# Eight experts as one straight program at fixed sizes, with one weight ring and transposed outputs

## The chip, the cores and the metric

The kernel runs on one core of one Trainium2 chip. The core has a matrix engine (TensorE, PE in the rows, with its weight loads as PEld), a vector engine (VectorE, DVE), a scalar engine (ScalarE, ACT), GpSimd (POOL) and SyncE (SP), which here only issues DMAs. The metric is the device time of one execution in microseconds. The kernel before took 626.72 us (median of three runs: 617.67, 628.06, 626.72).

## The reference, cut to what matters

Three layers follow one another on 1152 tokens of 512 features (2 batches of 576, 8 heads of 64):

```
attn = g * (phi(q) M_prev / phi(q) z_prev) + (1 - g) * causal_softmax(q k^T / 8) v

logits = x @ w_gate;  expert = argmax(logits);  gate = max of softmax(logits)
a token is kept if it is among the first 288 of its expert; else its output row is 0
out[i] = gate[i] * relu(x[i] @ w1[e]) @ w2[e]          # 8 experts, 512 -> 1024 -> 512

xn = x / sqrt(mean(x^2) + 1e-6) * rms_g
y  = (silu(xn @ w_gate2) * (xn @ w_val)) @ w_out        # 512 -> 1536 -> 512
```

All is float32. With the reference's default draw the experts have 14, 151, 0, 60, 1, 556, 8 and 362 tokens, so after the limit of 288 the sorted counts are 288, 288, 151, 60, 14, 8, 1, 0, together 810 rows. The rows of the third layer are these 810; the other tokens' output is 0.

## The kernel before, in words

**Precision.** Large products are made of three matmuls on a split into a high part (rounded to the matrix engine's fast float format, fp32r) and a low part (the rest): hi*hi, hi*lo, lo*hi (TERMS). For expert weights the split is a cast and a subtraction (`split`, L853 and L854). The weights of the third layer are read as 32-bit words in pairs (their high and low words) and put together by bit operations before the same split (`conv_steps`, L767 to L785): of one 1 MB matrix four pieces, each with three ACT, four DVE and one POOL instruction. Small products are plain float32 matmuls from the raw weights.

**Attention** (L188 to L712) is straight code with a written order; its end routes the tokens: each block's rows are scattered with a gate factor and a token number behind the 512 features into `disp`, a DRAM table with 288 rows for each expert. `rank` orders the experts by their counts on the DVE; the loads of expert weights take their addresses from registers on SP. Some weights are loaded (seven buffers of 1 MB, `wraw`) and two are split already here.

**Experts** (L1126 to L1317). There are eight positions in order of work: largest, smallest, second smallest, second largest, third smallest, third largest, and so on. For each position every engine reads a class number (the count rounded up to 0, 32, 64, 128, 160, 256 or 288 rows, and whether the next one is tiny) and jumps with `tc.Switch` (L1201) into the arm written for that class. An arm above 64 rows (`up_big`, L987; `down`, L1014) multiplies with split weights; the hidden layer comes out with its 1024 features on the partitions, the output with tokens on the partitions, by 128 rows and a tail of 32 (`down_tail`, `gather`). An arm of 32 or 64 rows (`tiny`, L941) uses float32 matmuls. What finishes an expert (`finish_y`, L1053: sum of squares, root, scaling, and a DMA to `comp`, the compact table of rows) is for most positions in a second switch after the arm (`finish_later`, L1067). Weights come through the seven buffers in an order of their own for each position (`uses`, `seq`, `ring`); three matrices of the third layer are loaded and converted inside expert arms (`extra`). The work of PE, DVE, ACT and POOL inside an arm is in written order.

**Third layer** (L1318 to L1487). It is one more switch, with an arm for each number of 64-row half blocks. 832 rows are in three chunks of 256, 256 and 320 columns. For each of six groups of 256 hidden features and each chunk, `gv` makes gate and value (48 matmuls a chunk and group), then `outp` multiplies into the output rows. Rows are read from `comp` (`x_in`), normalised, turned on PE (`x_turn`) and split. All engines but PE and SP are ordered here by a scheduler. Finished rows are scattered into the output by token number.

Of the kernel before, what the change touches and what calls it, by code (L numbers as in the profile page):

```python
# [22 lines left out]
def attn_moe_kernel(ctx, tc, q, k, v, M_prev, z_prev, beta, w_gate, w1, w2, cap, g_gate, g_val, g_out, rms_g, out):  # L23
# [21 lines left out]
    nc.gpsimd.memset(zrow[:, DM:DM + 1], 1.0)  # L45
# [11 lines left out]
    CW = DM + 2  # L57
    EB = 5
# [3 lines left out]
    comp = dram.tile([N + P * max(NBK, 2), CW], F32, name="comp")  # L62
# [33 lines left out]
    def rank(pk, erow):  # L96
# [5 lines left out]
        nc.vector.tensor_scalar(out=up, in0=ra, scalar1=-2.0, scalar2=float(2 * E - 1), op0=ALU.mult, op1=ALU.add)  # L102
        nc.vector.scalar_tensor_tensor(out=ra, in0=ra, scalar=2.0, in1=up, op0=ALU.mult, op1=ALU.min)
        nc.vector.tensor_scalar(out=up, in0=ra, scalar1=-2.0, scalar2=1.0, op0=ALU.mult, op1=ALU.add)
        nc.vector.scalar_tensor_tensor(out=up, in0=ra, scalar=2.0, in1=up, op0=ALU.is_lt, op1=ALU.mult)
        nc.vector.tensor_tensor(out=ra, in0=ra, in1=up, op=ALU.add)
# [11 lines left out]
    extra = {0: [0], 3: [1], 5: [2]}  # L118
    succ = lambda e: 2 if e == 0 else e + 1
    uses = [[] if e == 1 else [4 * e + 2, 4 * e + 3] + [4 * E + u for u in extra.get(e, [])] + ([4 * succ(e), 4 * succ(e) + 1] if e + 1 < E else []) for e in range(E)]  # L120
    seq = [0, 1] + [u for e in range(E) for u in uses[e]]
    early = seq[:NRAW]
    pos = {u: i for i, u in enumerate(seq)}
    SK = 4 * E + sum(len(z) for z in extra.values()) - len(seq)

    X2 = pos[4 * (E - 2) + 3]
    ring = [(X2 + j) % NRAW for j in (1, 2, 3, 4, 5, 0, -1)]

    def raw_tile(u):
        i = pos.setdefault(u, u - SK)  # L130
        if i < NRAW and i not in rawt:
            rawt[i] = wraw.tile([P, HALF], F32, tag="wr", name="wr")
        return rawt[i % NRAW if i < X2 + NRAW else ring[(i - X2 - NRAW) % NRAW]]

# [27 lines left out]
    wctx = ExitStack()  # L162
# [28 lines left out]
    ctx.enter_context(tc.manual_schedule(engines={mybir.EngineType.PE, mybir.EngineType.SP}))  # L191
    with ExitStack() as actx:
# [288 lines left out]
        def route(b, i, x):  # L481
# [39 lines left out]
            nc.vector.reciprocal(out=x[:n, DM:DM + 1], in_=r4[:n, 3:4])  # L521
# [89 lines left out]
        def act(z):  # L611
# [93 lines left out]
        for u in early[NRAW - 2:]:  # L705
            wl[u] = w_load(u // 4, u % 4) if u < 4 * E else m2_load(u - 4 * E)
# [7 lines left out]
    m2w = ctx.enter_context(tc.tile_pool(name="m2w", bufs=3, reuse_waits="tile"))  # L714
# [6 lines left out]
    sizes = sorted({min(s, cap) for s in [0, 32, 64, P] + [j * P + r for j in range(1, NBK) for r in (32, P)]})  # L721
    NS = len(sizes) - 1
    SM = 32
    NT = sum(s <= 2 * SM for s in sizes) - 1
    LO0 = sum(s < min(cap, -(-N // E)) for s in sizes)
    HI1 = sum(s < min(cap, N // E) for s in sizes)
    assert LO0 > NT
    arms = [[(c, t) for t in (False, True) for c in range(NS + 1)]] * E
    never = lambda e, c, t: e == 0 and c < LO0 or e == 1 and c > (NT if t else HI1)
    sthr = mc.tile([P, E, NS], F32, name="sthr")  # L730
    for j, s in enumerate(sizes[:-1]):
        nc.gpsimd.tensor_scalar(out=sthr[:, :, j], in0=ebase, scalar1=float(s), scalar2=None, op0=ALU.add)
    ccmp = pcmp.rearrange("p a b -> p (a b)")[:, :E * NS].rearrange("p (e s) -> p e s", e=E)

    rg_sb = mc.tile([P, DM], F32, name="rg_sb")
    nc.sync.dma_start(rg_sb, rms_g[None, :].to_broadcast([P, DM]))
    cnt = mc.tile([P, E], F32, name="cnt")
    off = mc.tile([P, E], F32, name="off")
    tmp = mc.tile([P, E], F32, name="tmp")
    tot = mc.tile([P, 1], F32, name="tot")  # L740
    ctl = mc.tile([P, 2, E], I32, name="ctl")
    ctt = mc.tile([P, 4], I32, name="ctt")
    nc.gpsimd.memset(eps, 1e-6)
    flg = mc.tile([P, E], F32, name="flg")
# [83 lines left out]
    with ExitStack() as mctx:  # L828
# [685 lines left out]
```

## Time and profile before

| what | value |
|---|---|
| median of the three runs | 626.72 us |
| lowest, highest run | 617.67, 628.06 us |
| profiled execution, first to last instruction | 621.6 us |
| PE, DVE, ACT, POOL busy | 77%, 55%, 44%, 28% of the span |

The profiled execution is one more run of its own; for it the span is the time that is listed, and it lies inside the range of the three runs. The rows below give times in us from the span's start. Attention ends near 199 us, the first matmul of the third layer starts at 420 us.

### The profile page before, as it was taken

Reading aid. Unit: us, or ns where it says so; the run is one execution under the profiler, and the core shown is the slowest. Engines: PE = TensorE matmul, PEld = TensorE weight load, DVE = VectorE, ACT = ScalarE, POOL = GpSimd, SP = SyncE. Lnnn points to the kernel's source line nnn. Section 1 sums busy time; section 2 is a strip of 40 time slices with the busy share of each in tenths; the row PEclk is TensorE's granted clock in tenths of the full one; section 3 lists DMA queues with packets and bytes.
Section 4 is the critical chain, followed back from the end, with each engine's and each line's share of the span. In section 5 each row is a group of like instructions: output and inputs, shape, how many; then the busy total and the mean of one; then the engine's idle time right before and its main releaser. Section 6 shows DMA issues by size and latency. Waiting matters only on the chain.

```text
span 621.6 us, 11099 instructions
## 1 busy us (share of the span) xinstructions
PE 478.9 (77%) x3753; PEld 399.2 (64%) x3754; DVE 342.5 (55%) x943; ACT 274.9 (44%) x704; POOL 173.0 (28%) x275
## 2 busy tenths in 40 slices
PE   7679999798984882455845683375998899999995
PEld 4568878687864751255534551234897788898993
DVE  6736754667575820217322460022799898989432
ACT  5736655465562620315322430123677565655210
POOL 3122321424162410224223420000146152434113
PEclk9879997898896996677975787668899999999998
DMA  9899695704964473463667443422965540000002
GB/s 170 159 289 235 148 223 117 155 2 112 322 220 128 137 251 73 158 196 135 210 180 224 147 144 95 116 65 64 388 213 172 198 152 37 1 2 1 1 35 76
DMA packets 76152, 89.33 MB, mean 144 GB/s; under 512 B 39862, under 2 KB 49078, under 8 KB 75873
## 3 DMA queue, kind: packets, MB, share of 16 engines
q1 hardware_dynamic: 73792, 81.25, 44.8%
q0 software_dynamic: 1936, 5.32, 2.5%
q14 instruction: 223, 1.82, 1.2%
q8 instruction: 57, 0.93, 0.8%
q10 hardware_dynamic: 144, 0.00, 0.0%
HBM read 61.90 MB, written 14.41 MB: 123 GB/s over the span
## 4 chain that ended last, share of the span: by engine, by line
issue 22%; DVE 16%; PE 9%; DMA 4%; ACT 4%; POOL 3%; SPq 1%; another core or an unknown queue 0%; ACTq 0%; DVEq 0%; POOLq 0%
DVE wr L774 3%; DVE t L769 3%; DMA wr<-in_moe_w 2%; POOL mlo L785 2%; PE gv L825 2%; DVE t L776 2%; DVE t L778 1%; DVE acc L1419 1%; DVE gh L1399 1%; DMA wr<-in_moe_w_gate 1%; PE z L1412 1%; PE keep L975 1%; DVE s L1396 1%; ACT t L767 1%; DVE wl L854 1%
## 5 line engine op out<-in xcount | busy, mean ns | idle before, releaser
L785 POOL TENSOR_TENSOR mlo<-t,mhi 128x256 fp32r<-128x256 f32 x72 | 66.2, 944 | 108.4 <-ACT mhi L784 83.3
L825 PE MATMUL gv<-XT,mhi 128*128 128x320 f32 (+1 forms) x384 | 82.2, 298 | 4.2 <-ACT s L1395 3.3
L999 PE MATMUL hpb<-xh,wh 128*128 128x288 f32 (+1 forms) x192 | 49.9, 350 | 36.1 <-issue 18.9
L825 PEld LDWEIGHTS gv<-XT,mhi 128*128 128x128 f32 x384 | 63.3, 189 | 7.4 <-ACT s L1395 5.0
L999 PEld LDWEIGHTS hpb<-xh,wh 128*128 128x128 f32 x192 | 40.1, 244 | 38.5 <-issue 19.6
L1412 PE MATMUL z<-mhi,gh 128*128 128x512 f32 (+1 forms) x168 | 60.5, 407 | 2.8 <-DVE acc L1419 1.3
L410 PE MATMUL s<-k,qT 128*128 128x256 f32 (+2 forms) x256 | 49.3, 318 | 10.5 <-DMA qT<-w 10.5
L443 DVE TENSOR_REDUCE nm<-s 128x1 f32<-128x384 f32 (+4 forms) x60 | 38.9, 648 | 33.2 <-PE s L413 19.5
L825 PE MATMUL gv<-XT,mlo 128*128 128x256 f32 (+1 forms) x192 | 56.7, 295 | 0.0
L479 PE MATMUL o<-rv,pt 128*64 128x65 f32 (+1 forms) x800 | 47.0, 240 | 0.0
L767 ACT ACTIVATE t<-wr 128x256 f32<-128x256 f32 x72 | 29.9, 440 | 38.3 <-DVE wr L774 34.6
L449 ACT ACTIVATE p<-s,nm 128x128 f32<-128x128 f32 (+4 forms) x80 | 42.9, 561 | 6.7 <-PE t L464 3.2
L410 PEld LDWEIGHTS s<-k,qT 128*128 128x128 f32 (+1 forms) x256 | 37.9, 195 | 12.2 <-issue 11.3
L479 PEld LDWEIGHTS o<-rv,pt 128*64 128x64 f32 (+1 forms) x800 | 37.2, 147 | 8.9 <-issue 5.2
L468 ACT COPY pt<-t 128x512 f32<-128x512 f32 (+2 forms) x48 | 23.9, 497 | 36.8 <-PE t L464 36.6
L464 PE MATMUL t<-ident,p 128*128 128x128 f32 (+2 forms) x240 | 37.9, 283 | 2.2 <-DVE phT L341 2.1
L1412 PEld LDWEIGHTS z<-mhi,gh 128*128 128x128 f32 (+1 forms) x168 | 30.9, 184 | 12.1 <-DVE xs L1419 1.9
L825 PE MATMUL gv<-xs,mhi 128*128 128x256 f32 x176 | 34.4, 287 | 4.3 <-DVE XT L1381 4.3
L825 PEld LDWEIGHTS gv<-XT,mlo 128*128 128x128 f32 x192 | 36.2, 189 | 1.0
L951 PE MATMUL hps<-wr,xf 128*32 128x256 f32 (+1 forms) x112 | 15.4, 607 | 26.3 <-issue 25.0
L774 DVE SCALAR_TENSOR_TENSOR wr<-wr,t 128x256 uint32<-128x256 uint32 x72 | 35.6, 526 | 0.1
L769 DVE TENSOR_SCALAR t<-wr 128x256 uint32<-128x256 uint32 x72 | 30.6, 455 | 8.7 <-POOL mlo L785 6.3
(287 smaller groups left out, 1073.8 us busy)
## 6 DMA issues: line engine op xcount, KB each, us to landing
wr<-in_moe_w SPq DMA_DIRECT2D x28, 1024.0 KB, 6.5
wr<-in_moe_w_gate SPq DMA_DIRECT2D x6, 1024.0 KB, 7.1
wr<-in_moe_w_val SPq DMA_DIRECT2D x6, 1024.0 KB, 9.5
wr<-in_moe_w_out SPq DMA_DIRECT2D x6, 1024.0 KB, 10.1
disp<-zrow SPq DMA_DIRECT2D x4, 1040.0 KB, 11.0
k<-w SPq DMA_DIRECT2D x8, 512.0 KB, 7.1
xs<-disp SPq DMA_DIRECT2D x12, 260.0 KB, 4.5
qT<-w SPq DMA_DIRECT2D x12, 256.0 KB, 6.5
```

Of the source, the lines that this page charges most:

```text
L410: nc.tensor.matmul(dst[:n, o0:o0 + c1 - c0], lhsT=st[b, i]["qT"][:, h, st[b, i]["off"]:st[b, i]["off"] + n], rhs=kT[b][half][j][:, h, k0:k ...
L443: nc.vector.tensor_reduce(out=m, in_=s.rearrange("p (g w) -> p g w", g=g)[:n, :, :ext], axis=AX.X, op=ALU.max, negate=True)
L449: nc.scalar.activation(out=p[:n, a * w:a * w + ext], in_=s[:n, a * w:a * w + ext], func=AF.Exp, bias=m[:, a:a + 1], scale=1.0)
L464: nc.tensor.transpose(tv[:kr, a * nk + j, :n], p[:n, a * w + j * P:a * w + j * P + kr], ident[:n, :n])
L479: nc.tensor.matmul(o[c:c + 64, h % 4], lhsT=pt[:kr, a + j, c:c + 64], rhs=vs[b, j][:kr, h], start=(j == 0), stop=(j == i))
L767: nc.scalar.activation(out=t1, in_=H.bitcast(F32), func=AF.Square)
L769: nc.vector.tensor_scalar(out=t2, in0=H, scalar1=0xC0000000, scalar2=None, op0=ALU.bitwise_and)
L774: nc.vector.scalar_tensor_tensor(out=H, in0=H, scalar=3, in1=t1.bitcast(U32), op0=ALU.logical_shift_left, op1=ALU.bitwise_and)
L785: nc.gpsimd.tensor_tensor(out=lo[:, s_], in0=f, in1=hi[:, s_].bitcast(F32), op=ALU.subtract)
L825: nc.tensor.matmul(pss[part], lhsT=W[wi][:, o:o + P], rhs=XT[:, a, k_, c0:c0 + n] if m0 else XT0[a][k_ // 2][:, k_ % 2, :n], start=(k_ == ...
L999: nc.tensor.matmul(ps[:, :un], lhsT=W[k_ // (KD // 2)][w][:, c:c + P], rhs=xh[:, a, k_, :un], start=(k_ == 0 and n_ == 0), stop=(k_ == KD ...
L1412: nc.tensor.matmul(zs[m][:nr], lhsT=h[:, a, r:r + nr], rhs=W[wi][:, fi * DM:(fi + 1) * DM], start=(fi == 0 and n_ == 0), stop=(fi == 1 and ...
```

## The change

The attention part stays, but for two details: the gate factor is multiplied into the row before it is scattered, and `rank` deals the positions anew. Positions are now large, small, large, small, large, small, and then two small ones: 1st, 8th, 2nd, 7th, 3rd, 6th, 4th, 5th in order of count. Each position has a fixed number of rows (`ROWS`), whatever its count. The three large ones and the five small ones are written one after the other without a switch; a small expert's steps are called between the steps of the large one ahead of it (hooks). What does not fit is done by one general arm behind a single flag (`overflow`). All 32 expert matrices and then the third layer's matrices pass through the ring of seven in one order (`pump`, `done`).

Outputs have their features on the partitions: `down` makes 128 features by n tokens, the sum of squares over features is a matmul with ones (`fin_norm`), and `fin_put` writes columns into `compT` and token numbers into `idsD`. The third layer reads its input turned already. Its first three matrices are converted after the last expert, into the buffers of the experts' split weights.

```diff
-    CW = DM + 2
-    EB = 5
+    ROWS = [min(cap, r) for r in (cap, 32, cap, 32, 192, 32, 64, 32)]
+    CPAD = cap + P
...
-            nc.vector.reciprocal(out=x[:n, DM:DM + 1], in_=r4[:n, 3:4])
+            nc.vector.reciprocal(out=r4[:n, 3:4], in_=r4[:n, 3:4])
+            nc.vector.tensor_scalar(out=x[:n, :DM], in0=x[:n, :DM], scalar1=r4[:n, 3:4], scalar2=None, op0=ALU.mult)
...
-    arms = [[(c, t) for t in (False, True) for c in range(NS + 1)]] * E
-    never = lambda e, c, t: e == 0 and c < LO0 or e == 1 and c > (NT if t else HI1)
...
+        def pump():
+            while loaded[0] < min(len(seq), 4 * E + NRAW) and loaded[0] - NRAW in gone:
+                u = seq[loaded[0]]
+                wl[u] = w_load(u // 4, u % 4) if u < 4 * E else m2_load(u - 4 * E)
+                loaded[0] += 1
+
+        def done(*us):
+            gone.update(us)
+            pump()
...
+                nc.scalar.copy(hi[:, s_], t[:, s_])
+                nc.vector.tensor_tensor(out=lo[:, s_], in0=t[:, s_], in1=hi[:, s_].bitcast(F32), op=ALU.subtract)
+                if j:
+                    done(u)
+                yield
...
+            for d in range(KD):
+                ps = ps_h.tile([P, 512], F32, tag="h", name="ypb")
+                for f in range(KF):
+                    c = (f % (KF // 2)) * DM + d * P
+                    for n_, (a, w) in enumerate(TERMS):
+                        nc.tensor.matmul(ps[:, :n], lhsT=W[2 + f // (KF // 2)][w][:, c:c + P], rhs=ht[:, a, f, :n], start=(f == 0 and n_ == 0), stop=(f == KF - 1 and n_ == 2))
+                nc.scalar.activation(out=sq[:, d, :n], in_=ps[:, :n], func=AF.Square)
+                nc.vector.tensor_scalar(out=yg[:, d, :n], in0=ps[:, :n], scalar1=rgT[:, d:d + 1], scalar2=None, op0=ALU.mult)
+                hook(d)
...
+        def fin_norm(e):
+            _, yg, n, pl, s = fin[e]
+            ps = ps_x.tile([P, 512], F32, tag="x", name="ssp")
+            nc.tensor.matmul(ps[:, :n], lhsT=onesf, rhs=s, start=True, stop=True)
+            nc.scalar.activation(out=s, in_=ps[:, :n], func=AF.Sqrt, scale=1.0 / DM, bias=eps)
+            nc.vector.reciprocal(out=s, in_=s)
+            nc.vector.tensor_tensor(out=yg, in0=yg, in1=s.unsqueeze(1).to_broadcast([P, KD, n]), op=ALU.mult)
...
+        def put(off_, row, n, yg):
+            nc.gpsimd.dma_start(compT.rearrange("(k p) n -> p k n", p=P)[:, :, bass.ds(off_, n)], yg)
+            nc.gpsimd.dma_start(idsD[bass.ds(off_, n), :], disp[bass.ds(row, n), DM + 1:DM + 2])
...
-            for a in tc.Switch({g_: cls_v[e] if nxt else end_v for g_ in AE}, len(arms[e])):
-                cls, flag = arms[e][a]
...
+        for e in BIGS:
+            t, nx, pv = e + 1, e + 2 if e + 2 in BIGS else None, e - 1 if e else None
+            bg = Steps(split(u) for u in (4 * e + 2, 4 * e + 3))
+            def up_hook(f):
+                if f == 0 and e:
+                    fin_norm(e - 2)
+                    fin_put(e - 2)
+                    fin_put(e - 1)
+                bg(1)
+                if f == 4:
+                    t_turn(t, xl[t][0], ROWS[t])
+            up(e, up_hook)
+            bg()
+            t_up(t, ROWS[t], raw4(t))
+            done(4 * t, 4 * t + 1)
+            sp = Steps(split(u) for u in (4 * nx, 4 * nx + 1)) if nx else Steps()
+            def down_hook(d):
+                if d == 0:
+                    t_mid(t, ROWS[t])
+                elif d == 1:
+                    t_down(t, ROWS[t], raw4(t))
+                    done(4 * t + 2, 4 * t + 3)
+                elif d == 2:
+                    t_fin(t, ROWS[t])
+                else:
+                    fin_norm(t)
+                if nx and d < len(tks(nx)):
+                    x_turn(nx, d)
+                sp(2 if d == 1 else 1)
+                if d == 3:
+                    fin_sum(e)
+            down(e, down_hook)
+            sp()
...
+        t_turn(6, xl[6][0], ROWS[6])
+        t_up(6, ROWS[6], raw4(6))
+        done(24, 25)
+        fin_norm(4)
+        fin_put(4)
+        w2ctx.close()
+        ovp = pool("ovp", 1)
+        xst = fbp.tile([P, KD, cap], F32, name="sq")[:, :, :2 * P]
+        nc.gpsimd.dma_start(xst, compT.rearrange("(k p) n -> p k n", p=P)[:, :, :2 * P])
+        fin_put(5)
+        t_mid(6, ROWS[6])
+        t_turn(7, xl[7][0], ROWS[7])
+        t_down(6, ROWS[6], raw4(6))
+        done(26, 27)
+        t_up(7, ROWS[7], raw4(7))
+        done(28, 29)
+        t_fin(6, ROWS[6])
+        t_mid(7, ROWS[7])
+        t_down(7, ROWS[7], raw4(7))
+        done(30, 31)
+        fin_norm(6)
+        fin_put(6)
+        t_fin(7, ROWS[7])
+        fin_norm(7)
+        fin_put(7)
...
+        for u in range(2):
+            Ms[u] = m2_conv(wl[4 * E + u], msets[u])
+        g01 = [ps_y[1 - fi].tile([P, 2, 2 * P], F32, tag="y", name="g0") for fi in range(2)]
+        gv_mm((0, (0, 2), 0), 2 * P, Ms, [g01[0][:, part] for part in range(2)], None)
...
+        for a in tc.Switch({g_: flag_v for g_ in AE}, 2, hint="over"):
+            if a:
+                overflow()
+        tc.switch_hint({g_: nb_v for g_ in AE}, 2 * MT - NH0 + 1, "nb")
+        gv_mm((0, (0, 2), 1), 2 * P, Ms, [g01[1][:, part] for part in range(2)], None)
+        Ms[2] = m2_conv(wl[4 * E + 2], msets[2])
...
+            for c in chunks[1:]:
+                c0, n = c[0] * P, ncol(c)
+                nc.sync.dma_start(stage(c), compT.rearrange("(k p) n -> p k n", p=P)[:, :, c0:c0 + n])
...
-        for a in tc.Switch(nb_v, 2 * MT):
+        for a in tc.Switch(nb_v, 2 * MT - NH0 + 1, hint="nb"):
```

The helpers `t_turn`, `t_up`, `t_mid`, `t_down` and `t_fin` are the steps of a small expert (`tiny` before, cut in five), `x_turn` and `up` are `x_turn_in` and `up_big` without their tails. How the change moves instructions, at two places:

The first is PE at the last two small experts (`hps` and `tps` are a small expert's hidden layer and output, `hx`, `xps`, `yx` turned tiles, `ssp` the sum of squares). Before, one of the arms of 32 rows:

```order
L1506 UNCONDITIONAL_BRANCH
L1201 BRANCH_PREFETCH_HINT
L1506 UNCONDITIONAL_BRANCH
L880 MATMUL xps<-ident,ht 128x128 x4
L951 MATMUL hps<-wr,xf 32x256 x16
L964 MATMUL hx<-ident,h 128x128 x2
L975 MATMUL keep<-wr,h 32x128 x32
L887 MATMUL xps<-ident,xs 128x128 x8
```

Now, from the end of the third large expert on:

```order
L931 MATMUL ssp<-ssum,onesf 128x32
L952 MATMUL xps<-ident,xs 128x64 x4
L965 MATMUL tps<-wr,xf 64x512 x8
L931 MATMUL ssp<-ssum,onesf 128x192
L976 MATMUL hx<-ident,h 128x128 x4
L952 MATMUL xps<-ident,xs 128x32 x4
L991 MATMUL tps<-wr,h 64x256 x16
L965 MATMUL tps<-wr,xf 32x256 x16
L1001 MATMUL yx<-ident,ysb 128x128 x2
L976 MATMUL hx<-ident,h 128x128 x2
L991 MATMUL tps<-wr,h 32x128 x32
```

A small expert's matmuls are the same; the branches around them are gone, and the two last small experts run side by side with no large one to fill their gaps.

The second is DVE at the conversion of the third layer's matrices (L769 to L778 before, L761 to L770 now). Before, inside the arm of a large expert, between the hidden layer's low parts (`ht`):

```order
L1010 SCALAR_TENSOR_TENSOR ht<-hpb,ht 128x256
L769 TENSOR_SCALAR t_4548<-wr 128x256
L769 TENSOR_SCALAR t_4553<-wr 128x256
L774 SCALAR_TENSOR_TENSOR wr<-wr,t_4547 128x256
L774 SCALAR_TENSOR_TENSOR wr<-wr,t_4552 128x256
L1010 SCALAR_TENSOR_TENSOR ht<-hpb,ht 128x256
L776 SCALAR_TENSOR_TENSOR t_4548<-wr,t_4548 128x256
L776 SCALAR_TENSOR_TENSOR t_4553<-wr,t_4553 128x256
L778 SCALAR_TENSOR_TENSOR t_4548<-wr,t_4548 128x256
```

Now, behind the last small expert's normalisation:

```order
L933 RECIPROCAL ssum<-ssum 128x32
L934 TENSOR_TENSOR tyg<-tyg,ssum 128x4x32
L1098 TENSOR_LOAD ctl
L1099 TENSOR_LOAD ctl
L1100 SWITCH_STRIDE
L1100 ISA
L1100 BRANCH_PREFETCH_HINT
L1104 TENSOR_TENSOR xh<-sq,xh 128x2x256 x2
L761 TENSOR_SCALAR t_4473<-wr 128x256
L761 TENSOR_SCALAR t_4478<-wr 128x256
L766 SCALAR_TENSOR_TENSOR wr<-wr,t_4472 128x256
```

Three conversions, which lay in the expert stage, now stand behind it.

## Rows read from the trace of the kernel before

**Rows 1.** Busy time by stage: experts, then the third layer in two stretches.

```profile
core 0: us, PE busy (x) PEld busy (x) DVE busy (x) ACT busy (x) POOL busy (x), PEclk, DMA share, GB/s
...
199.00:420.00 221.00, 132.28 (x854) 98.67 (x856) 68.53 (x112) 62.91 (x169) 50.38 (x62) 0.76 0.48 154
420.00:463.00 43.00, 34.47 (x221) 31.22 (x218) 27.68 (x71) 25.08 (x64) 9.88 (x18) 0.92 0.67 239
463.00:581.00 118.00, 112.25 (x716) 100.46 (x715) 107.75 (x269) 72.82 (x195) 47.79 (x49) 1.00 0.22 75
```

**Rows 2.** Waits, 199 to 420 us: engine, line, releaser, us in total, times, longest.

```profile
PEld hps L951 <- issue: 33.8, 22, 12.6
```

**Rows 3.** Chain of waits, 199 to 420 us: shares by line.

```profile
by line: issue 42.5%; DMA wr<-in_moe_w 6.9%; PE keep L975 3.2%; DVE wl L854 2.7%; SPq L868 2.3%; PE yps L975 2.2%; PE hpb L999 1.8%; DMA comp<-xn 1.5%; ACT h L1056 1.4%; PE keep L1023 1.3%; PE yps L1023 1.3%; DVE t L769 1.1%; DVE ht L1010 1
```

**Rows 4.** Timeline, expert stage begins: start, us, instruction, idle before and its releaser.

```profile
192.98 0.95 DVE L890 TENSOR_TENSOR xh<-xps,xh 128x512 fp32r<-128x512 f32 x2 [0.16 <-ACT xh L889]
...
198.98 0.60 PE L999 MATMUL hpb<-xh,wh 128*128 128x288 f32 x1 [5.67 <-issue]
...
202.97 0.38 PE L999 MATMUL hpb<-xh,wl 128*128 128x288 f32 x1
```

**Rows 5.** PE timeline: 18 matmuls of 288 columns, 21 of 192, four transposes.

```profile
213.60 0.43 PE L999 MATMUL hpb<-xh,wh 128*128 128x288 f32 x2
...
216.00 0.43 PE L999 MATMUL hpb<-xh,wh 128*128 128x288 f32 x2
...
216.53 0.60 PE L880 MATMUL xps<-ident,xs 128*128 128x128 f32 x4
...
343.18 0.39 PE L999 MATMUL hpb<-xh,wh 128*128 128x192 f32 x2
...
345.53 0.39 PE L999 MATMUL hpb<-xh,wh 128*128 128x192 f32 x2
```

**Rows 6.** PE timeline: small experts of 32 and 64 rows, third layer's first matmul.

```profile
246.64 3.64 PE L951 MATMUL hps<-wr,xf 128*32 128x256 f32 x32 [12.14 <-issue]
...
261.41 3.48 PE L975 MATMUL keep<-wr,h 128*32 128x128 f32 x64
...
402.72 6.23 PE L951 MATMUL hps<-wr,xf 128*64 128x512 f32 x16 [7.56 <-issue]
...
415.34 5.06 PE L975 MATMUL yps<-wr,h 128*64 128x256 f32 x32
...
420.33 0.39 PE L825 MATMUL g<-xs,mhi 128*128 128x256 f32 x1
```

**Rows 7.** DVE timeline: half of a split with POOL idle.

```profile
258.97 1.22 DVE L854 TENSOR_TENSOR wl<-wr,wh 128x1024 fp32r<-128x1024 f32 x1
```

**Rows 8.** Weight DMAs (count, KB, us to landing), and a stretch full of loads.

```profile
wr<-in_moe_w SPq DMA_DIRECT2D x28, 1024.0 KB, 6.5
...
432.00:448.00 16.00, 14.14 (x84) 12.78 (x84) 10.54 (x28) 9.55 (x26) 2.25 (x6) 0.79 0.98 357
```

**Rows 9.** Stages as in rows 1, only instructions on the raw weights (`wr`).

```profile
420.00:463.00 43.00, 2.07 (x16) 1.44 (x12) 19.48 (x50) 5.38 (x14) 0.43 (x3) 0.92 0.67 239
463.00:581.00 118.00, 0.00 (x0) 0.00 (x0) 76.88 (x197) 19.16 (x47) 0.00 (x0) 1.00 0.22 75
```

**Rows 10.** PE timeline: first matmul of the sixth and last group.

```profile
581.23 0.28 PE L825 MATMUL gv<-xs,mhi 128*128 128x256 f32 x1
```

**Rows 11.** ACT and PE behind the last switch: idle before, and releaser.

```profile
430.44 1.28 ACT L1395 ACT_TABLE_LOAD   x1 [7.99 <-issue]
...
L1378 PEld LDWEIGHTS xgp<-ident,wr 128*128 128x128 f32 x8 | 0.9, 141 | 3.5 <-issue 3.5
```

**Rows 12.** Result rows' DMAs: count, KB, us to landing.

```profile
comp<-xn POOLq DMA_DIRECT2D x6, 64.2 KB, 2.5
```

**Rows 13.** Matmuls by shape, 199 to 445 us: 192 columns, small experts of 32.

```profile
L999 PE MATMUL hpb<-xh,wh 128*128 128x192 f32 x64 | 17.6, 370 | 15.0 <-DVE ht L1010 7.7 <-issue 7.3
...
L951 PE MATMUL hps<-wr,xf 128*32 128x256 f32 x96 | 9.2, 549 | 18.8 <-issue 17.4 <-ACT gi L1058 1.4
```

More of the change, by code (lines that the diff above doesn't have):

```diff
@@ L117, in attn_moe_kernel @@
     rawt = {}
[L118 to L127, printed above, removed]
+    early = list(range(NRAW))
     def raw_tile(u):
[L130 to L133, printed above, removed]
+        if u < NRAW and u not in rawt:
+            rawt[u] = wraw.tile([P, HALF], F32, tag="wr", name="wr")
+        return rawt[u % NRAW]
     def w_load(e, part, t=None):
@@ L806, in m2_conv @@
         return hilo
[L808 removed]
     ps_y = [ctx.enter_context(tc.tile_pool(name=f"ps_y{j}", bufs=1, reuse_waits="tile", space=PSUM)) for j in range(2)]
[L810 to L813 removed]
     TERMS = ((0, 0), (0, 1), (1, 0))
+    xh = xh[0]
+    XT0 = xh[:, :, :, :2 * P]
+    msets = [[W[s][a][:, c * UE:(c + 1) * UE] for a in range(2)] for s in range(2) for c in range(2)]
+    Ms = {}
     def gv_mm(u, n, M, pss, XT):
@@ L841, in attn_moe_kernel @@
+        w2ctx = ExitStack()
+        wsp = w2ctx.enter_context(tc.tile_pool(name="wsp2", bufs=1, reuse_waits="tile"))
         W.extend([wsp.tile([P, HALF], F32R, name=f"w{a}{s}") for a in ("h", "l")] for s in range(2, 4))
         ht = htp.tile([P, 2, KF, cap], F32R, name="ht")
-        SPLIT = (("ap", "vv"), ("ap", "av"))
-        SPLIT0 = (("ap", "ap"), ("ap", "ap"))
         SC = HALF // 2
-        def split(u, plan=None, ahead=True):
+        BIGS = [e for e in range(E) if e % 2 == 0 and e <= 4]
@@ new lines, in attn_moe_kernel, with __init__, __call__ @@
+        ld = nc.values_load_multi_w_load_instructions
+        class Steps:
+            def __init__(self, gens=()):
+                self.g = list(gens)
+            def __call__(self, n=99):
+                while n and self.g:
+                    if next(self.g[0], 0) == 0:
+                        self.g.pop(0)
+                    else:
+                        n -= 1
+        seq = [*range(4 * E), *(4 * E + u for u in range(3 * NG))]
+        gone, loaded = set(), [NRAW]
+        def pump():
[3 more added lines that the diff above has]
+                loaded[0] += 1
@@ L1123, in attn_moe_kernel @@
-        mw = [[m2w.tile([P, UE], F32R, name=n_) for n_ in ("mhi", "mlo")] for _ in range(3)]
-        Ms = dict(enumerate(mw))
-        def background(gens):
-            gens = list(gens)
-            def bg(n):
-                while n and gens:
-                    if next(gens[0], 0) == 0:
-                        gens.pop(0)
-                    else:
-                        n -= 1
-            return bg
-        ld = nc.values_load_multi_w_load_instructions
+                    nc.tensor.matmul(yps[i * nr:(i + 1) * nr, :dw], lhsT=htf[:, hc:hc + nr], rhs=ws[2 + f // (KF // 2)][:, o + i * dw:o + (i + 1) * dw], start=(f == 0), stop=(f == KF - 1))
```

713 lines of the change are left out of this document (215 added, 498 removed).

## The prediction

> **What bounds the kernel now.** I read the stages first, then the waits and the chain of the middle stage, then single timelines. By stage [rows 1], PE is busy 132 of 221 us in the experts at a mean granted clock of 0.76, and 147 of 161 us in the third layer up to its last group, at 0.92 and 1.00. So the loss lies in the experts. There the longest waits name no engine and no transfer: PE's weight load at L951 alone waited 33.8 us for "issue" [rows 2], which is time in which an engine that waits for nothing has no instruction to run, and "issue" is 42.5% of the chain of that stage, about 94 us [rows 3]. The waits stand where an arm begins: 5.67 us before the first arm's first matmul [rows 4], 12.14 and 7.56 us before small experts [rows 6]. Attention, written straight, is not of this kind. The third layer is different: of its first 161 us DVE is busy 135 [rows 1], 96 of them on instructions that touch the raw weights [rows 9], the conversions of 15 matrices, or 6.4 us each. PE and DVE are both nearly full there.
>
> Does the data fit the fixed sizes? The reference's counts, sorted, are 288, 288, 151, 60, 14, 8, 1, 0; the rows now are 288, 288, 192, 64 and four times 32. The trace ran one large expert on 192 columns (64 matmuls of one kind, two thirds of the 96 of an expert) and three small ones of 32 rows (96 records, 32 each) [rows 13], and one of 64 [rows 6]. So nothing overflows and the general arm is skipped. An empty expert, skipped before, now costs a run of 32 rows.
>
> **The change, part by part.**
>
> *Start.* The turned input is ready at 193.9 us [rows 4], and the next matmul need not wait for a switch. The gate factor adds one DVE instruction to the last block. I start at 194.5 instead of 199.0.
>
> *Large experts.* Up and down are 96 matmuls each. At full clock three of 288 columns take 0.40 us (18 in 2.40), so 0.133 each, and 21 of 192 take 2.35, so 0.112 [rows 5]. Two experts of 288: 384 x 0.133 = 51.1 us. One of 192: 192 x 0.112 = 21.5 us.
>
> *Small experts.* 32 rows took 3.64 + 3.48 = 7.1 us, 64 rows 6.23 + 5.06 = 11.3 [rows 6]. Four and one make 39.8, the upper end, since the longer rows followed idle time, at the lower clock; at twice that speed it would be 20. Between full matmuls the clock should hold, behind gaps not. Nearest are the rows themselves; I take 35.
>
> *Turned tiles.* A set of four transposes is 0.60 us [rows 5]. Five for the next large inputs, three a small expert, and eight short matmuls with ones, which the trace doesn't have and which I count as two thirds of a set: 5 + 15 + 5 = 25 sets' worth at most, 15 us, at least 8, since sets of 32 columns are shorter. I take 13.
>
> *Exposed.* Before, the first 4 us of the stage (198.98 to 202.97) ran at half the pace [rows 4]: 2 us. One microsecond for each large expert's handover. The last two small experts have nothing beside them, so their evictions show: 4 us. Sum 9.
>
> Together 51.1 + 21.5 + 35 + 13 + 9 = 129.6: the last small expert's output ends at 194.5 + 129.6 = 324 us, where it now ends at 420.3 [rows 6].
>
> *What must stay hidden.* Splitting is all on ACT and DVE now, with POOL idle: 1.22 us of DVE for half a matrix [rows 7], eight halves a large expert, 9.8 us beside some 36 us of PE; its cover could shrink to a quarter before it showed. The weights: 26 MB still to come in 130 us, 200 GB/s; 357 GB/s were reached while loads queued [rows 8]. A load goes out when the matrix seven places ahead is released, which is half an expert before its use, 15 us or more against 6.5 to landing [rows 8]. SP is in order, so a held load also holds the next input rows, which are wanted one expert later. The result DMAs wait for one another on POOL, which has nothing else to do. 64 KB took 2.5 us [rows 12]; the new ones have 512 short rows, and I put 3 to 8 us on each. Behind the last small expert there are two, beside conversions that last longer. If conversions got short, these would be next.
>
> *Conversions.* This is what the change gives back. Three matrices were converted inside expert arms; now the first starts after the last expert is normalised and the first 256 columns are split, 5 us after PE (an estimate: a dozen short DVE and ACT instructions in turn, and the first tile's split of about 1.4 by rows 4). So conversions begin at 329. From there to the start of the last group DVE has its 135.4 us of now [rows 1], plus 3 x 6.4 = 19.2, less about 3 for the normalising that goes: 152. It was busy 91% of the long stretch (107.75 of 118) [rows 1], so 166; and it passes two switches. Last group at 329 + 166 + 7 = 502. PE gives about the same: the first group, held by four conversions, 55 us, and four groups at some 29.5 (118 us for four from 463 to 581) [rows 1]. From the last group's first matmul, 581.2 [rows 10], to the end of the span are 40.4 us, which stay. End: 542.4 us.
>
> *The two switches left.* The flag's and the third layer's. Before, ACT waited 7.99 us behind the last one and PE 3.5 [rows 11]. Both are announced earlier now than their jump, so I take PE's 3.5 each; the ends are 0 and 8. The Trainium skill, "Runtime: NRT & Kernel Launch", section "Instruction fetch mechanics", says that a taken branch to code outside the window already fetched must wait for a fetch, while straight code streams in unseen. By that rule both switches, one of which jumps over the whole general arm, would cost their full 8, and the sum would be 551. No row here shows a switch announced that early.
>
> **Sum.** The experts lose 96 us, the third layer, counted from the last small expert, gains 17: 218 instead of 201. The span goes from 621.6 to 542.4, by 12.7%. The profiled span stands 0.8% under the median of the three runs; taken as a share of that median, 626.72 x 0.873 = 547 us.
>
> **Rivals.**
>
> *Both switches cost in full*: nine more, span 551, time 556. For it: 8 us waits on ACT behind the last switch [rows 11]. Against: the hints. This is also what the skill's rule gives. Chance 0.13.
>
> *The weight stream becomes the bound*: if each of 26 loads had to land alone, 26 x 6.5 = 169 us from 195.5, and the last small expert would end at 368 rather than 324; time 591. For it: one ring in strict order, and more bytes. Against: 357 GB/s with several in flight. Chance 0.08.
>
> *The clock stays low*: at the 0.76 of now [rows 1] the 121 us of PE work become 159; time 585. For it: every handover is a gap. Against: the stage's low clock belongs to the stretches of waiting that go; where PE was dense, it was 1.00. Chance 0.06.
>
> *DVE packs better*: the third layer at 152 us without idle time, and small experts near 22: 27 less, time 520. Chance 0.07.
>
> *Slower: an expert doesn't fit.* The general arm then reloads 4 MB for each of six positions and does 22 pieces one after the other. A piece of 64 rows costs at least 11.3 us [rows 6] plus its handovers, so 250 us and more: about 800. It decides as soon as one count passes its rows. The counts above speak against it. Chance 0.03.
>
> *It saves nothing*: the waits called "issue" may move rather than go, if fetching, not jumping, is what is slow; then only the order changes. Against: attention and the third layer's arm run for over 150 us with next to none. Chance 0.03.
>
> **How the numbers follow.** The forecast, 547, has 0.60; its own range is 525 to 570, from small experts between 20 and 40, turned tiles between 8 and 15, switches between 0 and 8 each and DVE at 88 to 100%. For 8 in 10 I widen it toward the better packing below and toward the two rivals near 590 above: 518 to 588. About two per cent is what a measurement tells from no change. Faster by more than that are all cases but the last two: 0.94; within it 0.03; slower 0.03.
>
> **What would show it.** First up matmul near 194.5; a PE share above 85% between there and the last small expert's output, whose end says 324 or not; no wait for "issue" above 3 us in it; no weight DMA as the releaser of PE or ACT. Behind it a PE gap of some 10 us while the first two matrices are converted, a first group of some 55 us, then groups of 29 to 30. If the gap at either switch is 8 us, the first rival is right. If ACT's copies wait for weight DMAs, the second. If DVE is not above 85% in the first three groups, the way the third layer was counted is wrong. A time above 600 would mean the fixed program doesn't stream.

## The result and the profile after

The changed kernel took **561.43 us** (median of four runs, 557.99 to 564.19) against 627.39 for the kernel before in the same comparison: ratio 0.903, 95% interval 0.893 to 0.914, so 9.7% faster. Forecast: 547, range 518 to 588. The profiled execution's span is 562.7 us (forecast for the span: 542.4). That is 20 us more than forecast, and the sum of errors of opposite sign: the experts were 10.6 us shorter than forecast, what follows them 28.5 longer. The medians below are of all runs of a kernel, the ratios of those in the faster of its two states, and the profiled executions of "again", "nohint" and "seqsmall" were in the slower one.

By stage, columns as in [rows 1]: experts from the first product to the end of the last small expert's second product; from there to the first conversion; to the first product of the last switch's arm; to the last group; the rest.

```profile
196.80:315.80 119.00, 110.81 (x1078) 97.72 (x1078) 61.84 (x107) 45.16 (x92) 7.91 (x12) 0.96 0.91 279
315.80:339.00 23.20, 1.31 (x7) 0.87 (x5) 3.44 (x9) 3.12 (x9) 3.86 (x6) 0.56 0.86 244
339.00:378.00 39.00, 18.76 (x63) 14.95 (x64) 24.97 (x65) 21.00 (x52) 10.10 (x14) 0.56 0.39 119
378.00:522.20 144.20, 133.46 (x851) 121.95 (x850) 126.36 (x312) 88.11 (x236) 59.80 (x60) 0.98 0.23 76
522.20:562.70 40.50, 32.47 (x205) 28.93 (x204) 12.88 (x25) 4.96 (x12) 6.93 (x7) 0.94 0.12 43
```

The first row answers to the first of [rows 1]: 119 us instead of 221, PE busy 93% of it instead of 60%, at a granted clock of 0.96 instead of 0.76. From the last small expert to the last group it is 206.4 us (23.2 + 39.0 + 144.2), where it was 160.9 (420.33 to 581.23, [rows 6, 10]): 45.5 of the 102 us come back there. In the second row PE, DVE and ACT do next to nothing for 23 us.

Of the 102 us that the experts gained, 21.5 are busy time of PE (132.3 to 110.8, at the higher clock) and 80.5 its idle time (88.7 to 8.2). Before, PE's waits in that stage were led by these:

```profile
PE hps L951 <- issue: 25.0, 3, 12.1
PE hpb L999 <- issue: 18.9, 3, 7.3
PE hx L964 <- ACT h L959: 18.3, 4, 7.3
```

Six waits for "issue" make 43.9 us (the first, 5.7 us, lies just ahead of the stage). Now PE has none there.

The timeline of PE shows the small experts; each line is one product of one expert.

```profile
196.76 0.40 PE L899 MATMUL hpb<-xh,wh 128*128 128x288 f32 x1 [0.35 <-ACT xh L889]
...
212.70 3.61 PE L965 MATMUL tps<-wr,xf 128*32 128x256 f32 x32 [2.26 <-DMA wr<-in_moe_w]
...
249.16 1.93 PE L965 MATMUL tps<-wr,xf 128*32 128x256 f32 x32
...
301.00 3.65 PE L965 MATMUL tps<-wr,xf 128*64 128x512 f32 x16 [0.46 <-ACT xf L954]
...
306.79 3.67 PE L991 MATMUL tps<-wr,h 128*64 128x256 f32 x32 [0.37 <-ACT h L978]
...
313.85 1.95 PE L991 MATMUL tps<-wr,h 128*32 128x128 f32 x64 [0.52 <-ACT h L978]
...
522.25 0.28 PE L815 MATMUL gv<-xh,wh 128*128 128x256 f32 x1
```

An up product of 32 rows is 1.93 us where it was 3.64 [rows 6]; only the first, behind the one wait for a weight DMA (2.26 us), still takes 3.61, at a granted clock of 0.53 (1.00 in the 3.7 us after it). The last row is the first matmul of the last group.

The idle 23 us, first POOL, where the result DMAs are issued (the first and the last L937 of these belong to positions 4 and 7; the read between them at L1081 fetches the first 256 turned columns), then DVE and ACT:

```profile
308.34 0.79 POOL L937 DMA_DIRECT2D compT<-yg  x1 [20.84 <-DVE yg L934]
...
315.52 0.77 POOL L1081 DMA_DIRECT2D sq<-compT  x1 [5.82 <-issue]
327.33 0.75 POOL L937 DMA_DIRECT2D compT<-tyg  x1 [11.03 <-DMA sq<-compT]
...
334.60 0.79 POOL L937 DMA_DIRECT2D compT<-tyg  x1 [6.00 <-DMA compT<-tyg]
...
337.70 0.77 POOL L937 DMA_DIRECT2D compT<-tyg  x1 [1.77 <-DMA compT<-tyg]
```

```profile
334.07 0.29 DVE L1006 TENSOR_TENSOR tyg<-yx,rgT 128x128 f32<-128x128 f32 x1 [16.50 <-DMA compT<-tyg]
...
338.96 0.49 DVE L761 TENSOR_SCALAR t<-wr 128x256 uint32<-128x256 uint32 x2
...
357.15 0.50 DVE L761 TENSOR_SCALAR t<-wr 128x256 uint32<-128x256 uint32 x2 [4.48 <-issue]
...
372.02 0.76 DVE L1211 TENSOR_TENSOR s<-g,s 128x256 f32<-128x256 f32 x2 [4.40 <-ACT s L1210]
```

```profile
370.31 1.28 ACT L1210 ACT_TABLE_LOAD   x1 [5.45 <-issue]
```

Each result DMA waits until the one before it, or the read, has landed; the last small expert's scaling waits 16.5 us for a buffer that such a DMA reads; DVE's conversions stand behind that. The two waits for "issue" at 357 and 370 us are the two switches.

### The profile page after: what moved, and what is told of

It is laid out like the page before. It is cut to its first block, busy times and chain, and to the rows that moved or that the text cites. A ratio compares the mean times of both kernels' runs of the same rounds, so it can differ in the third digit from the quotient of the medians.

```text
span 562.7 us, 10987 instructions
## 1 busy us (share of the span) xinstructions
PE 471.2 (84%) x3959; PEld 410.2 (73%) x3960; DVE 354.7 (63%) x959; ACT 270.2 (48%) x661; POOL 142.5 (25%) x232
## 5 line engine op out<-in xcount | busy, mean ns | idle before, releaser
L777 POOL TENSOR_TENSOR wl<-t,wh 128x256 fp32r<-128x256 f32 x48 | 43.9, 935 | 62.6 <-ACT wh L776 62.6
L815 PE MATMUL gv<-XT,wh 128*128 128x320 f32 (+1 forms) x256 | 55.6, 301 | 4.3 <-ACT s L1210 4.3
L433 DVE TENSOR_REDUCE nm<-s 128x1 f32<-128x384 f32 (+4 forms) x60 | 38.8, 647 | 29.9 <-PE s L403 21.5
L815 PEld LDWEIGHTS gv<-XT,wh 128*128 128x128 f32 x256 | 43.1, 192 | 5.7 <-ACT s L1210 4.9
L469 PEld LDWEIGHTS o<-rv,pt 128*64 128x64 f32 (+1 forms) x800 | 39.5, 150 | 10.6 <-issue 5.9
L899 PE MATMUL hpb<-xh,wh 128*128 128x288 f32 (+1 forms) x192 | 41.3, 307 | 0.4 <-ACT xh L889 0.4
L917 PE MATMUL ypb<-ht,wh 128*128 128x288 f32 (+1 forms) x192 | 38.8, 293 | 0.0
L815 PE MATMUL gv<-XT,wl 128*128 128x256 f32 (+1 forms) x128 | 38.4, 300 | 0.0
L760 ACT ACTIVATE t<-t,kc 128x256 int32<-128x256 f32 x72 | 35.2, 503 | 0.7
L1211 DVE TENSOR_TENSOR s<-gv,s 128x256 f32<-128x256 f32 (+1 forms) x34 | 14.9, 439 | 28.6 <-PE gv L815 28.6
L761 DVE TENSOR_SCALAR t<-wr 128x256 uint32<-128x256 uint32 x72 | 26.3, 398 | 10.2 <-issue 4.5
L917 PEld LDWEIGHTS ypb<-ht,wh 128*128 128x128 f32 x192 | 31.0, 189 | 1.9 <-issue 1.8
L777 POOL TENSOR_TENSOR ml<-t,mh 128x256 fp32r<-128x256 f32 x24 | 25.3, 1077 | 24.5 <-ACT mh L776 24.5
```

The lines of the kernel that those rows point to most:

```text
L433: nc.vector.tensor_reduce(out=m, in_=s.rearrange("p (g w) -> p g w", g=g)[:n, :, :ext], axis=AX.X, op=ALU.max, negate=True)
L469: nc.tensor.matmul(o[c:c + 64, h % 4], lhsT=pt[:kr, a + j, c:c + 64], rhs=vs[b, j][:kr, h], start=(j == 0), stop=(j == i))
L760: nc.scalar.activation(out=t1.bitcast(I32), in_=t1, func=AF.Sign, scale=-1.0, bias=thr)
L761: nc.vector.tensor_scalar(out=t2, in0=H, scalar1=0xC0000000, scalar2=None, op0=ALU.bitwise_and)
L777: nc.gpsimd.tensor_tensor(out=lo[:, s_], in0=f, in1=hi[:, s_].bitcast(F32), op=ALU.subtract)
L815: nc.tensor.matmul(pss[part], lhsT=W_[wi][:, o:o + P], rhs=XT[:, a, k_, c0:c0 + n] if m0 else XT0[:, a, k_, :n], start=(k_ == 0 and n_ == ...
```

## The experiments

All runs by stage, from their traces, in us: start of the first expert product; experts; to the first conversion; to the arm's first product on later columns; to the last group; and the span. Attention's length differs between executions (the first product starts between 190 and 201), so stages are compared, and times through the ratio to the kernel before.

| run | start | experts | to conversion | to arm | to last group | span | median | ratio (95%) |
|---|---|---|---|---|---|---|---|---|
| changed | 196.8 | 119.0 | 23.2 | 38.7 | 144.6 | 562.7 | 561.4 | 0.903 (0.893 to 0.914) |
| again | 197.1 | 119.9 | 25.2 | 39.0 | 144.3 | 566.2 | 559.0 | 0.892 (0.887 to 0.897) |
| tyg4 | 191.7 | 118.9 | 14.4 | 47.6 | 144.5 | 557.8 | 557.7 | 0.891 (0.886 to 0.895) |
| convfirst | 192.9 | 120.3 | 5.1 | 55.8 | 144.3 | 559.0 | 558.4 | 0.891 (0.886 to 0.897) |
| noswitch | 192.2 | 118.4 | 25.8 | 32.0 | 144.2 | 552.0 | 552.0 | 0.875 (0.868 to 0.883) |
| nohint | 197.6 | 119.0 | 21.5 | 39.5 | 143.4 | 561.7 | 553.6 | 0.891 (0.886 to 0.897) |
| jumps | 193.8 | 135.9 | 20.4 | 38.8 | 143.4 | 573.2 | 578.3 | 0.935 (0.927 to 0.943) |
| jumpshint | 201.0 | 140.9 | 20.8 | 38.3 | 143.7 | 585.5 | 585.1 | 0.939 (0.931 to 0.947) |
| seqsmall | 196.5 | 127.7 | 23.5 | 38.8 | 143.4 | 570.5 | 568.6 | 0.908 (0.900 to 0.916) |
| threeops | 193.3 | 119.6 | 24.8 | 33.2 | 141.8 | 553.6 | 550.8 | 0.881 (0.877 to 0.886) |
| lodve | 190.1 | 119.1 | 5.1 | 43.3 | 143.4 | 541.6 | 542.0 | 0.869 (0.865 to 0.873) |
| best | 195.0 | 116.9 | 13.8 | 36.8 | 143.5 | 546.4 | 544.7 | 0.872 (0.868 to 0.877) |
| lodve3 | 190.4 | 122.6 | 5.9 | 40.9 | 143.4 | 543.7 | 542.6 | 0.876 (0.872 to 0.879) |

**again.** 

> The changed kernel once more, as the base for the runs beside it. Both theories: span 556 to 564 us; the last small expert's second product ends near 316 us, the first conversion starts near 338 us, the last group near 521 us.

The stages agree with the first profile to 1 or 2 us; 0.892 is the base below.

**Do jumps cost what the experts gained?** Straight code gets three switches back:

```
+ for a in tc.Switch({g_: flag_v for g_ in (PE, ACT, DVE)}, 2):
+     if a:   # 200 matmuls, 100 ACT copies, 100 DVE copies
```

**jumps.** 

> The straight experts get three switches back: ahead of the second and third large expert and of the last two small ones, PE, ACT and DVE each jump over an arm (200 matmuls, 100 copies, 100 copies) that is never run. No announcement. Theory A: jumps are what the experts lost before; each costs PE 4 to 8 us, so the experts end 12 to 24 us later and the time rises as much. Rival: the jump is cheap and the old arms lost their time in something else (waits between engines at an arm's end, loads in another order): below 5 us for all three.

The waits of PE from 190 to 345 us (engine, line, releaser; us in total, times, longest), and behind them DMA and clock of the three stretches:

```profile
PE hpb L899 <- issue: 13.6, 2, 7.0
PE xps L952 <- issue: 6.9, 1, 6.9
PE hpb L899 <- DVE ctl L747: 4.5, 1, 4.5
```

```profile
228.00:235.00 7.00, 0.00 (x0) 0.00 (x0) 3.17 (x5) 0.33 (x3) 0.00 (x0) 0.76 0.89 306
269.00:275.00 6.00, 0.00 (x0) 0.00 (x0) 3.17 (x5) 0.36 (x3) 0.00 (x0) 0.80 1.05 384
305.00:311.70 6.70, 0.00 (x0) 0.00 (x0) 2.30 (x5) 0.13 (x2) 0.00 (x0) 0.63 0.97 367
```

Three jumps, 20.5 us of idle PE, and the experts are 16.9 us longer: 6.5 us of other waits (4.2 for DVE, 2.3 for a DMA) are gone, and PE's work took 2.8 us more at a mean clock of 0.90. The time is 0.043 of the kernel before up, some 26 us. A part of that, 4.5 us, is not the jumps': the flag is now read at the start, and the first product waited for it; the other few us lie within the interval. Theory A holds: 6.8 us of waiting a jump, 5.6 net of what it hides, in the stage from which the change took them. The Trainium skill, "Runtime: NRT & Kernel Launch", section "Instruction fetch mechanics", says that a taken branch out of the fetched window waits for a fetch; these waits agree with it.

**nohint.** 

> Both switches stay, their early announcements go. Theory A: an announcement hides a part of the fetch at the target; without it the two switches cost 8 us each, as the last one did before the change, instead of some 4.5 and 5.5, and the time rises by 5 to 7 us. Rival: the announcements come too late to do anything, or what is waited for is not a fetch: within 2 us of the changed kernel.

```diff
- tc.switch_hint({g_: flag_v for g_ in AE}, 2, "over")
- tc.switch_hint({g_: nb_v for g_ in AE}, 2 * MT - NH0 + 1, "nb")
```

Equal: 0.891 against 0.892. PE's wait at the first switch was 5.3 us (5.7 with the announcement), ACT's at the second 5.4 in both.

**jumpshint.** 

> The same three switches, each announced at the start of the second product of the expert before, some 15 us ahead. Theory A: the announcement fetches the target, which leaves 3 to 4 us a jump: half of what the switches without announcement add. Rival 1: it hides all, within 2 us of the changed kernel. Rival 2: it hides nothing, equal to the run without announcements.

```diff
  if d == 0:
+     tc.switch_hint({g_: flag_v for g_ in JE}, 2, f"j{e + 2}")
```

```profile
PE hpb L899 <- issue: 14.1, 2, 7.6
PE xps L952 <- issue: 11.0, 1, 11.0
```

Rival 2: the three waits were 7.6, 6.5 and 11.0 us, against 7.0, 6.6 and 6.9 without announcement. In this kernel an announcement bought nothing at five places. Why, these runs don't tell.

**noswitch.** 

> Without the general arm and both switches: the arm for 13 half blocks stands as straight code, right for these inputs alone. Theory A: DVE's 10.9 us of idle time from 354 to 372 us are the two switches' price, and DVE sets what follows, so the span falls by 8 to 10 us, to 553. Rival: the time is the start of the third layer's pipeline (table load, first gate product at the low clock), not the jumps: below 3 us. Forecast's count: 7 us for both.

```diff
- for a in tc.Switch(nb_v, 2 * MT - NH0 + 1, hint="nb"):
-     arm(a + NH0)
+ arm(13)
```

From the first conversion to the arm 32.0 us instead of 38.7: 6.7 us for both, what the forecast counted (7), and a little less than expected here. The median fell by 7.0, the ratio by 0.017, which would be some 10 us; its interval is too wide to tell them apart.

**seqsmall.** 

> Of the small experts at positions 1, 3 and 5 the transposes, the second product and the normalisation move from between the pieces of the large expert's second product to its end, one after the other. Theory A: the chain product, copy, transpose, copy, product stands open at each of the three, some 3 to 4 us, and the experts end 9 to 12 us later. Rival: PE's queue has other work at these places (turning the next rows) and the weight loads are ahead, so that straight code alone made the gain: below 3 us.

```diff
- if d == 0:  t_mid   elif d == 1:  t_down   elif d == 2:  t_fin   else:  fin_norm
+ if d == 3:  t_mid; t_down; t_fin; fin_norm
```

Experts 127.7 instead of 119.0, time up by 0.016, some 10 us. PE's idle time grew from 8.2 to 13.1 us, and the same 1078 records were busy 114.5 us instead of 110.8, at a mean granted clock of 0.93 instead of 0.96. So putting small steps between large ones is worth about 9 us.

**tyg4.** 

> Four buffers instead of two for the small experts' scaled outputs; nothing else. Theory A: the 16.5 us in which the last small expert's scaling waits for a result DMA are a buffer wait, and conversions on DVE decide the time of the third layer. Then the scaling starts at about 317.5 us instead of 334.1, the conversions start when the first 256 turned columns have landed, near 328 instead of 338, and the whole ends some 9 us earlier: span 553. Rival B: what is late is the transfers themselves (weights of the third layer and result DMAs on one crowded stretch of 376 GB/s), so that the buffer is only where it shows: conversions start after 335, gain below 3 us. Rival C: conversions start earlier but PE sets the rest: the last group moves by less than 4 us.

```diff
- yg = ftp.tile([P, KD, 64], F32, name="tyg")
+ yg = ftp.tile([P, KD, 64], F32, name="tyg", bufs=4)
```

**convfirst.** 

> Four such buffers, and the first conversion is put ahead of the split of the first 256 turned columns, so that it needs only its own weights. Theory A: it starts when the gate matrix has landed, issued at 304.7 and 16.5 us on its way, so near 321 us; 16 us earlier than 338, and all of it is kept: span 546. Rival B (crowded transfers): the gate matrix lands as late as the turned columns, near 327, gain 9. Rival C (PE sets the rest): conversions 16 us earlier, last group less than 6 us earlier.

```diff
+ Ms[0] = m2_conv(wl[4 * E], msets[0])
  for k_ in range(0, KD, 2):   # split of XT0
  ...
- for u in range(2):
-     Ms[u] = m2_conv(wl[4 * E + u], msets[u])
+ Ms[1] = m2_conv(wl[4 * E + 1], msets[1])
```

Both do what they should, and both gain nothing. DVE in the second of them, and POOL:

```profile
318.31 0.49 DVE L761 TENSOR_SCALAR t<-wr 128x256 uint32<-128x256 uint32 x2 [1.33 <-DMA wr<-in_moe_w_val]
...
341.72 1.55 DVE L761 TENSOR_SCALAR t<-wr 128x256 uint32<-128x256 uint32 x2 [15.09 <-POOL wl L777]
```

```profile
324.95 0.75 POOL L937 DMA_DIRECT2D compT<-tyg  x1 [11.63 <-DMA sq<-compT]
...
333.19 0.79 POOL L937 DMA_DIRECT2D compT<-tyg  x1 [6.96 <-DMA compT<-tyg]
...
339.04 0.76 POOL L937 DMA_DIRECT2D compT<-tyg  x1 [4.53 <-DMA compT<-tyg]
...
340.97 2.88 POOL L777 TENSOR_TENSOR wl<-t,wh 128x256 fp32r<-128x256 f32 x4 [0.63 <-issue]
```

The first conversion starts 18 us sooner behind the experts, and the second stands still for 15.1 us, because the last instruction of a conversion's piece (`wl`, L777) is POOL's, and POOL is held by result DMAs until 340. The buffer wait had only covered this one. None of the three theories had it: A's start of the conversions came true, its gain didn't; C's small gain came true, but the wait is POOL's and not PE's.

**lodve.** 

> As the run with the first conversion ahead, and the subtractions of the first two conversions are DVE's instead of POOL's. Theory A: the buffer wait was only the outer cover; what holds the third layer is POOL's queue, where the conversions' subtractions stand behind result DMAs that wait for one another (the second conversion stood still from 323 to 342 us). With them on DVE both conversions run from 318 to about 336 without a hole, and 13 to 16 us of the span go: 545. Rival (PE sets the rest): the conversions end earlier but the last group moves by less than 5 us. Rival (weights): the second conversion waits for its matrix until after 330, gain 6 us or less.

```diff
- nc.gpsimd.tensor_tensor(out=lo[:, s_], in0=f, in1=hi[:, s_].bitcast(F32), op=ALU.subtract)
+ low.tensor_tensor(...)   # low = nc.vector for matrices 0 and 1, else nc.gpsimd
```

This stands on top of convfirst and its four buffers. 542.0 us, 0.869 against 0.891 for convfirst: some 14 us gained by the ratio, 16 by the medians, with an edit that gives DVE more work. From the last small expert to the arm it is now 48.5 us; it was 62.0 and 60.9 in the two runs before. POOL's queue is shown as what held this stage.

**best** (lodve, and the general arm's switch ahead of the first conversion). 

> As the run with the subtractions on DVE, and the switch over the general arm stands right behind the last result DMA, ahead of the first conversion instead of behind the second, where ACT and DVE wait for the first matrix anyway and PE has nothing to do; no announcement. Theory A: of its 4 to 6 us about 3 are hidden, 3 us less than that run. Rival: the jump holds all engines as long at the new place, since the conversions start when it is done: within 1 us.

```profile
325.22 0.43 ACT L759 ACTIVATE t<-wr 128x256 f32<-128x256 f32 x1 [10.28 <-issue]
```

The rival: no gain. At its old place the jump cost ACT 4.1 us, here 10.3, right behind the load of the flag.

**lodve3** (the third conversion's subtractions on DVE too). 

> As the run with the subtractions of the first two conversions on DVE (542.0 us), with those of the third there too. In that run POOL's own jump over the general arm stood behind the result DMAs, so that POOL came to the third conversion's subtractions only at 348 us, and DVE waited 6.8 us for a buffer that they read. Theory A (POOL's queue is still what ends last): that wait goes, the arm's conversions begin some 5 us earlier and so does all behind them: 537. Rival: ACT and PE, which wait for the second switch until about 347, hold the arm's first chunk just as long: 540 to 542.

```profile
354.46 0.76 DVE L1214 TENSOR_TENSOR gh<-s,gh 128x256 fp32r<-128x256 f32 x2 [0.45 <-ACT gh L1213]
```

The rival again: 542.6 us against 542.0, by the ratio 0.876 against 0.869. From the last small expert to the arm it is 46.8 us, 1.7 less than in lodve, and the experts before it were 3.5 longer in this execution. DVE no longer waits for POOL, but what it computes for the arm's first chunk comes at 354 us, behind ACT's wait at the second switch (4.1 us) and its table load. Neither this run nor "best" is faster than lodve.

**threeops.** 

> The changed kernel with one of the four DVE instructions of every conversion left out (the one that brings in the top bits of the low word, so the last three bits of the weights are missing). Theory A: DVE sets the pace of the third layer's groups while there are conversions, 33 to 34 us each against some 25 of PE: about 1.6 us less for each of 15 matrices, 16 to 22 us of the span, until PE sets the pace. Rival: PE sets it already, or the chain between engines inside a chunk: below 6 us.

```diff
- nc.vector.scalar_tensor_tensor(out=t2, in0=L, scalar=29, in1=t2, op0=ALU.logical_shift_right, op1=ALU.bitwise_or)
```

From its arm to the last group:

```profile
370.90:512.60 141.70, 133.97 (x853) 121.86 (x852) 113.19 (x253) 88.30 (x237) 48.41 (x60) 0.98 0.23 77
```

DVE is busy 113.2 us instead of 126.4, and the stretch is 2.8 us shorter. A further 5.5 us come from ahead of the arm. The ratio fell by 0.011, some 7 us, where theory A asked for 16 to 22 and the rival for less than 6: DVE's time as a whole is not what the groups take. Nor is PE's alone. By group, from the second to the fifth, first the changed kernel, then this run:

```profile
393.24:428.33 35.09, 30.99 (x187) 27.60 (x186) 34.45 (x88) 27.31 (x73) 20.84 (x18) 0.95 0.51 167
428.33:461.38 33.05, 28.91 (x188) 26.13 (x186) 32.72 (x86) 22.46 (x62) 14.00 (x16) 1.00 0.30 108
461.38:494.08 32.70, 30.20 (x188) 27.48 (x186) 30.17 (x72) 19.52 (x53) 14.31 (x16) 0.95 0.00 1
494.08:522.25 28.17, 28.17 (x187) 26.04 (x186) 14.46 (x33) 6.64 (x17) 3.23 (x4) 1.00 0.00 1
```

```profile
386.39:421.74 35.35, 31.25 (x187) 27.42 (x186) 33.16 (x76) 28.94 (x80) 16.37 (x20) 0.95 0.61 208
421.74:455.70 33.96, 30.75 (x187) 27.43 (x186) 27.36 (x63) 21.18 (x58) 12.46 (x16) 0.95 0.12 42
455.70:484.50 28.80, 28.39 (x188) 26.05 (x187) 24.44 (x56) 18.18 (x49) 9.46 (x12) 1.00 0.00 1
484.50:512.65 28.15, 28.15 (x187) 26.00 (x186) 13.57 (x29) 7.12 (x18) 3.25 (x4) 1.00 0.00 1
```

The fifth group, in which little is left to convert, is all PE: 28.2 us. The three before it take 4.5 to 6.9 us more in the changed kernel; DVE is 92 to 99% busy in them, and PE waits 4.0, 4.1 and 2.4 us there until ACT has read earlier products (`s`, L1210). With a quarter of the conversions' DVE instructions gone only the fourth became shorter. So DVE converts ahead for as long as it has something to convert, and the groups in which it converts most are longer than PE needs; whether that comes from DVE, from ACT's part of the conversions or from the steps between them was not tried.

## Why the prediction was right, and where not

The sign and the mechanism were right as far as the runs go: PE's six waits for "issue" at the start of an arm, 43.9 us, are gone, and jumps put back bring such waits back. The terms of the sum against the trace (forecast, measured):

| term | forecast | measured | difference |
|---|---|---|---|
| first expert product | 194.5 | 196.8 | +2.3 |
| experts | 129.6 | 119.0 | -10.6 |
| to the first conversion | 5 | 23.2 | +18.2 |
| first conversion to last group | 173 | 183.3 | +10.3 |
| rest | 40.4 | 40.5 | +0.1 |

The differences sum to 20.3, the error of the span.

- *Small experts* are the experts' error. 35 us were taken; the products (L965 and L991) are busy 13.1 + 11.6 = 24.7 us, near the end (20) that assumed full clock. Nearest rows had been rows behind idle time; with PE never idle for long, the price at 1.2 GHz was met once, in the first (3.61 us at a clock of 0.53). What is left for large experts, handovers and turned tiles, 94.3 us, is their sum (94.6).
- *To the first conversion* is the step that failed. The text had the result DMAs "beside conversions that last longer", with POOL having "nothing else to do". In the trace the conversions wait for them: the last expert's scaling needs a buffer that position 5's result DMA reads, and that DMA stands behind the read of the first 256 columns, which held POOL for 11.0 us. The price of a result DMA, 3 to 8 us, was about right (6.6, 2.5 and 6.1 us to landing); the read between them was not counted. Nor was it that the last instruction of every conversion piece is POOL's subtraction, queued behind those DMAs. In the changed kernel this second wait does not show (POOL is free 2 us before its first subtraction), but it took all that tyg4 and convfirst had gained, until lodve removed it too.
- *First conversion to last group.* DVE's work there was forecast at 152 us and is 24.97 + 126.36 = 151.3. What went wrong is what it was divided by, the 91% of the groups before. By group, the first took 54.3 us from the first conversion on (forecast 55), but the four after it 129.0 instead of 118: the same amount of DVE work as before, 111.8 us against 107.75 [rows 1], now crowds into three of them, and these three are longer than PE needs. threeops shows that less DVE work alone gives little of that back.
- *Switches.* 7 us forecast, 6.7 by the stages of noswitch. The reason given (announced early) is refuted by nohint and jumpshint; the first rival, which counted 8 each, was wrong in size, for DVE waited 4.5 us and PE 5.75 at the first switch, ACT 5.45 at the second.
- *Other rivals.* The weight stream ended one wait of PE, 2.26 us; the clock was 0.96 in the experts, not 0.76; nothing overflowed. Of the signs named in advance, the PE share above 85% (93%) and no wait of PE, DVE or ACT for "issue" above 3 us in the experts came true. DVE above 85% in the first three groups came true for their sum (87% from the first product on) and proved nothing. The PE gap behind the experts was some 25 us instead of 10, and groups of 29 to 30 us did not come true.

The jumps put back cost 6.8 us of waiting each, and PE's six waits for "issue" before were 7.3 on average. That all of the 94 us under "issue" [rows 3], those of ACT and DVE among them, were jumps of this kind was not tried.

## What to carry to other kernels

A switch in the middle of a dense stage cost PE 6.5 to 11.0 us here; small experts run at a fixed size as straight code were cheaper than arms that fit them. Before calling a DMA hidden, read what else its issuing engine has queued behind it and who waits for the buffer that it reads; an idle engine that waits in order is a busy one. And a busy share near 90% is no proof of a bound when the work can run ahead: take some of it away and see, group by group, before naming the other engine.

## What was not expected of the hardware

A jump's price varied with the place, and in these rows it does not follow the traffic. The first three rows cover a wait of ACT each, 4.1 and 5.4 us at the two switches of the changed kernel and 10.3 in "best"; the last covers the 11.0 us of PE in "jumpshint":

```profile
353.60:357.00 3.40, 1.48 (x5) 1.18 (x5) 0.00 (x0) 0.00 (x0) 0.66 (x1) 0.50 0.27 38
364.90:370.30 5.40, 1.44 (x7) 1.15 (x6) 0.90 (x4) 0.00 (x0) 1.12 (x2) 0.82 0.96 349
315.00:325.00 10.00, 0.00 (x0) 0.00 (x0) 0.61 (x2) 0.00 (x0) 0.77 (x1) 0.50 0.93 271
313.30:324.20 10.90, 0.00 (x0) 0.00 (x0) 2.42 (x5) 0.25 (x2) 0.00 (x0) 0.59 0.68 253
```

The cheapest wait has the least traffic (0.27), but at 0.93 to 0.96 there are 5.4 and 10.3 us, the longest has 0.68, and PE in "jumps" waited 6.6 to 7.0 us at 0.89 to 1.05. No run changed the traffic alone, so what sets the price stays open. A hint ahead of a switch made no measured wait shorter.
